# Banded attention followed by a mixture of experts on one core: another opening, with other places, queues and rounds for the loads and the attention stages

## The chip, the core and the metric

The program runs on one core of a Trainium2 chip. The core has five engines, each with its own instruction stream, in order: TensorE (PE in the profile), VectorE (DVE), ScalarE (ACT), GpSimd (POOL) and SyncE (SP, which here only issues DMAs). They meet through semaphores, and transfers run on 16 DMA engines. The metric is device time in microseconds of one execution; the median of several is compared.

## The reference

`q`, `k` and `v` are 4 batches x 8 heads x 576 positions x 64. Heads 0 to 3 see a plain band of 32 positions, heads 4 to 7 a band of 128 with every fourth position:

```python
scores = scale * np.matmul(q, k.transpose(0, 1, 3, 2))
mask_plain = (rel >= 0) & (rel < window)
mask_dil = (rel >= 0) & (rel < window * dilation) & (rel % dilation == 0)
scores = np.where(masks[None, :, :, :], scores, -1000000000.0)
scores = scores - np.max(scores, axis=-1, keepdims=True)
attn = np.exp(scores)
attn = attn / (np.sum(attn, axis=-1, keepdims=True) + 1e-09)
return np.matmul(attn, v)
...
p = domain_probs / (domain_probs.sum(-1, keepdims=True) + 1e-09)
for e in range(E):
    h = np.maximum(x @ w1[e], 0.0)
    out += p[:, e:e + 1] * (h @ w2[e])
```

The attention's output is `x`, 2304 rows of 512 (row = batch and position, column = head and 64). Four experts have `w1` of 512 x 1024 and `w2` of 1024 x 512. All is float32.

## The kernel before

**Attention.** A group (b, p, i) is batch b, pair of heads p (0 and 1 plain, 2 and 3 dilated) and third i of the positions; there are 48. The host sorts positions of the dilated heads so that theirs is a plain band too. `load_qk` brings a group's q [128 x 192] and k [128 x 224] (96 and 112 KB), `load_v` the v windows of a step's groups [128 x 2 x 6 x 64] (192 KB a group). The groups are worked in 25 steps, the first two of one group and the others of two. A step goes through these stages, one in a round n of the main loop, at its lag: `s_qk` (lag 0, PE: 24 small products a group into a PSUM bank each), `s_max` (0, DVE: adds the mask, negates, and takes the row's extreme, three a group, line 285), `s_sub` (1, POOL), `s_exp` (1, ACT), `s_sum` (2, DVE: row sum over 65 columns, the last of which holds 1e-9, and reciprocal), `s_norm` (2, POOL: the product into a tile `pb`), `s_tr` (3, PE: three turns into one bank; ACT copies it out as `pts`, line 340), `s_av` (4, PE: 24 products a group into a bank each; ACT copies them into `x`, line 372). The tuple `stages` (line 378) sets in which order a round issues them: values, turn, scores on PE. The four PSUM places of tag `pa` are taken in rotation by scores, turns and values.

**Experts.** x is cut into three blocks of 768 rows, each in two chunks i of 384 (0 to 5), and w1 and w2 into 16 pieces of 512 KB (`u`). Each float32 operand is held as a high and a low part of a reduced type (`split`: ACT writes the high part, DVE or POOL the difference; `hh`, `hl` for the activations), and a product takes three matmuls in their place. For a visit (u, m) the first product is Strassen's: seven products instead of eight, for which the splits of sums and differences of x (`x_sums`, line 207, DVE, in place in x; `x_part`, the parts B11 to T4) and of w1 (`w1_sums`, POOL) are needed. A visit is a generator that issues 13 pieces: `mm1_b` gives five (S2, S1, S3, S4, A22) on the PSUM banks x and y, then come the next visit's first product in y, three pieces of `mm2` (second half of the rows), the next visit's second product in x, and three `mm2` of the first half. Each `mm2` piece ends in a pass of DVE that adds it into `acc` (line 495). The next visit's A12 product and the last of its five, A22 with T4, both need their bank to be free of what DVE reads of it. There are 47 such visits. Ahead of them stands piece 0 of block 0, which is done in the plain way (`plain`), in two halves of seven pieces each, since the second half of the block's rows exists later; `pause("open")` stands between the two.

**The main loop** (line 713) issues in each round n the loads, the stages, the splits that the table `when` has for n, the loads of weights, and then: below START (10) six filler matmuls (`dummies`, `wt`, which compute nothing and take the same two PSUM banks as `mm2`), from START to OPEN (15) two pieces of the experts, or six fillers while they pause, and from OPEN on PACE (12) pieces. Behind each piece `step()` issues one instruction's worth of the tasks in `queue` (splits and sums of weights and x), which `prepare` fills; `need` issues at once all that is left of a task. START is the round behind the last stage of those groups that block 0's first half needs, OPEN that of its second half. When attention is over, `begin()`, called once in each visit behind its three pieces of the second half, closes attention's tiles and opens wider ones for the experts, and prepares block 2's remaining parts (`x_sums` of chunks 4 and 5 among them). Where the visit that follows is the last of block 0, `need(x_sums, 5)` (line 563) asks for these.

**Queues.** All loads of q, k, the masks and the weights are issued by SP; v of batches 0 and 1 by ACT (line 254), v of batches 2 and 3 by SP; the tile of v has three places, those of q and k six. The shares (`probs`) are loaded as [128 x 18 x 4], and `weigh` normalises them into `pn`.

The functions that the change touches, with what calls them:

## Time and profile before

| | |
|---|---|
| median of 3 executions | 851.78 us (851.03 to 853.73) |
| the profiled execution | 848.25 us |
| its span, first to last instruction | 846.2 us |
| what lies around the span | 2.05 us |
| mean granted clock of TensorE | 0.995 |
| PE busy | 825.4 us, 98% |
| DVE, ACT, POOL busy | 57%, 38%, 48% |
| moved by DMA | 59.17 MB, 70 GB/s over the span |

The span runs from the profile's first instruction to its last; the time of an execution is 2.05 us longer. A share is busy time over the span, a mean over stages that differ. The page also cuts the span into 40 slices of 21 us: PE has 8, 6, 9 and 8 tenths in the first four slices and 9 or more in all later ones but the last, and the transfers' engines have 8, 9 and 8 tenths in the first three and 4 or less behind them.

### The profile page before, as it was taken

The page shows a single profiled execution, that of the slowest core. Times are in us where ns is not written, and L with a number is a line of the kernel's source. Part 1 is how long each engine was busy: PE and PEld are TensorE (multiplying, and loading weights), DVE is VectorE, ACT ScalarE, POOL GpSimd, SP SyncE. Part 2 cuts the span into 40 slices and gives each one's busy share as a digit, 9 for nine tenths or more (in the row PEclk, how much of TensorE's full clock was granted, in tenths as well). Part 3 has the DMA queues.
Part 4 walks back from the last instruction along what each step waited for, and adds up shares of the span by engine and source line. Part 5 has one row for each costly group of instructions (what it writes and reads, how often), then busy time and mean ns, then how long its engine had stood idle before and what let it go on. Part 6 is the DMA issues. An engine that isn't in the chain of part 4 may idle for free.

```text
span 846.2 us, 15635 instructions
## 1 busy us (share of the span) xinstructions
PE 825.4 (98%) x6219; PEld 728.9 (86%) x6219; DVE 482.4 (57%) x1015; ACT 319.5 (38%) x761; POOL 404.6 (48%) x484
## 2 busy tenths in 40 slices
PE   8698999999999999999999999999999999999998
PEld 5477788888888898898898898998998998988986
DVE  4566666568565559645545545555555455455554
ACT  2345544345444455433233242242242232232321
POOL 3466977667676678832332342341341342242210
PEclk9999999999999999999999999999999999999999
DMA  8983432342321221400100101101001001010003
GB/s 230 226 209 90 144 100 90 96 141 76 96 87 51 76 75 50 146 30 26 50 25 26 50 26 35 40 26 50 26 26 51 25 27 50 26 40 12 0 26 125
DMA packets 51464, 59.17 MB, mean 70 GB/s; under 512 B 5952, under 2 KB 40896, under 8 KB 51392
## 3 DMA queue, kind: packets, MB, share of 16 engines
q1 hardware_dynamic: 47936, 53.46, 20.7%
q10 hardware_dynamic: 3456, 4.72, 2.3%
q8 instruction: 49, 0.80, 0.4%
q14 instruction: 23, 0.19, 0.1%
HBM read 53.45 MB, written 4.72 MB: 69 GB/s over the span
## 4 chain that ended last, share of the span: by engine, by line
PE 90%; POOL 3%; DVE 2%; DMA 2%; ACT 1%; issue 1%; SPq 0%; ACTq 0%; POOLq 0%; DVEq 0%
PE m L487 45%; PE m1x L389 23%; PE m1y L389 17%; PE po L356 2%; PE sc L271 1%; PE wt L685 1%; DMA k_s<-kT 1%; PE pt L336 1%; DVE hl L413 1%; DVE xl_T L120 1%; DMA q_s<-qT 0%; POOL g2l L120 0%; POOL g1l L120 0%; DMA v_s<-vw 0%; DVE acc L495 0%
## 5 line engine op out<-in xcount | busy, mean ns | idle before, releaser
L495 DVE SCALAR_TENSOR_TENSOR acc<-m,pn,acc 128x512 f32<-128x512 f32 x270 | 201.8, 749 | 132.6 <-PE m L487 132.3
L487 PE MATMUL m<-w2h,hh 128*128 128x512 f32 x576 | 226.8, 394 | 2.8 <-DVE acc L495 2.3
L487 PE MATMUL m<-w2l,hh 128*128 128x512 f32 x576 | 225.5, 391 | 0.0
L120 POOL TENSOR_TENSOR g2l<-r,g2h 128x256 fp32r<-128x256 f32 x124 | 93.3, 780 | 240.9 <-PE m L487 212.1
L487 PE MATMUL m<-w2h,hl 128*128 128x512 f32 x576 | 178.7, 391 | 0.1
L407 ACT ACTIVATE hh<-s 128x384 fp32r<-128x384 f32 x94 | 49.4, 526 | 248.2 <-DVE s L430 197.8
L487 PEld LDWEIGHTS m<-w2h,hh 128*128 128x128 f32 x576 | 108.1, 188 | 25.4 <-DVE acc L495 4.9
L487 PEld LDWEIGHTS m<-w2h,hl 128*128 128x128 f32 x576 | 108.1, 188 | 24.2 <-DVE hl L413 0.6
L487 PEld LDWEIGHTS m<-w2l,hh 128*128 128x128 f32 x576 | 108.2, 188 | 20.1
L120 POOL TENSOR_TENSOR w2l<-r,w2h 128x512 fp32r<-128x512 f32 x62 | 80.7, 1323 | 45.1 <-ACT w2h L117 44.7
L120 POOL TENSOR_TENSOR g1l<-r,g1h 128x256 fp32r<-128x256 f32 x93 | 69.0, 762 | 68.7 <-ACT g1h L117 68.7
L446 DVE TENSOR_TENSOR s<-m1x,s 128x384 f32<-128x384 f32 x47 | 26.2, 558 | 104.2 <-PE m1x L389 102.6
L439 ACT ACTIVATE u<-m1x 128x384 f32<-128x384 f32 x47 | 23.1, 491 | 144.5 <-PE m1x L389 144.5
L413 DVE SCALAR_TENSOR_TENSOR hl<-s,hh 128x384 fp32r<-128x384 f32 x94 | 60.8, 647 | 28.1 <-ACT hh L407 28.1
L389 PE MATMUL m1x<-xh_T,g2h 128*128 128x384 f32 x156 | 53.0, 340 | 1.8 <-DVE s L430 1.8
L389 PE MATMUL m1x<-xl_T,g2h 128*128 128x384 f32 x156 | 52.8, 338 | 0.0
L389 PE MATMUL m1x<-xh_T,g2l 128*128 128x384 f32 x156 | 52.5, 337 | 0.0
L117 ACT ACTIVATE g2h<-r 128x256 fp32r<-128x256 f32 x125 | 43.4, 406 | 3.9 <-POOL r L149 3.9
L389 PE MATMUL m1y<-xl_B,g2h 128*128 128x384 f32 x128 | 43.1, 336 | 0.0
L389 PE MATMUL m1y<-xh_B,g2h 128*128 128x384 f32 x128 | 43.0, 336 | 0.0
L389 PE MATMUL m1y<-xh_B,g2l 128*128 128x384 f32 x128 | 42.9, 335 | 0.0
L285 DVE CUSTOM_DVE_ANT_0 sm<-sc,mask 128x64 f32<-128x64 f32 x144 | 23.0, 222 | 33.9 <-PE sc L271 27.4
(91 smaller groups left out, 1499.8 us busy)
## 6 DMA issues: line engine op xcount, KB each, us to landing
r<-w SPq DMA_DIRECT2D x64, 512.0 KB, 3.4
k_s<-kT SPq DMA_DIRECT2D x48, 112.0 KB, 3.8
v_s<-vw ACTq DMA_DIRECT2D x24, 192.0 KB, 4.5
q_s<-qT SPq DMA_DIRECT2D x48, 96.0 KB, 4.1
v_s<-vw SPq DMA_DIRECT2D x24, 192.0 KB, 4.0
out<-acc SPq DMA_DIRECT2D x18, 256.0 KB, 2.0
mask<-masks SPq DMA_DIRECT2D x1, 192.0 KB, 4.6
pw<-probs SPq DMA_DIRECT2D x1, 36.0 KB, 6.6
```

The costliest lines, as they stand in the source:

```text
L117: nc.scalar.activation(out=hi, in_=src, func=AF.Copy)
L120: lo_eng.tensor_tensor(out=lo, in0=src, in1=hi.bitcast(F32), op=ALU.subtract)
L271: nc.tensor.matmul(banks[swap][o:o + QB, i * KB:(i + 1) * KB], q_s[h, c0:c0 + QB], k_s[h, c0:c0 + KB], start=True, stop=True, skip_group_c ...
L285: nc.vector.tensor_tensor_reduce(out=sm[:, i * len(gs) + k, :KB], in0=banks[k][:, i * KB:(i + 1) * KB], in1=mask[:, which[blk if p < NP // ...
L356: nc.tensor.matmul(po[k][64 * j:64 * j + 64, o:o + QB], v_s[rows, j, 2 * i + half, :], ts_[rows, c:c + QB], start=True, stop=True,)
L389: nc.tensor.matmul(bank, w[:, k], x[:, k], start=(first and k == 0 and i == 0), stop=(last and k == 1 and i == 2), skip_group_check=True,)
L407: nc.scalar.activation(out=hi, in_=src, func=AF.Relu)
L413: nc.vector.scalar_tensor_tensor(out=lo, in0=src, scalar=0.0, in1=hi.bitcast(F32), op0=ALU.max, op1=ALU.subtract)
L439: nc.scalar.activation(out=u2, in_=x, func=AF.Copy)
L446: nc.vector.tensor_tensor(out=s5, in0=x, in1=s5, op=ALU.add)
L487: nc.tensor.matmul(po, h, w, start=(n == 0 and x == 0), stop=(n == 3))
L495: nc.vector.scalar_tensor_tensor(out=acc, in0=po, scalar=pn[:, tt, e:e + 1], in1=acc, op0=ALU.mult, op1=ALU.add,)
```

## The change

There are 24 steps of two groups. `LAG` is 3: in its own round a step now has scores, maxima, subtraction and exponential, in the next the sum and the product, then the turn, then the values; a round issues scores, values, turn on PE. After the steps that the first half of block 0 needs, and after those that its second half needs, GAP = 3 rounds have no scores (rounds 5 to 7 and 13 to 15), in which the earlier steps' later stages go on. START becomes round 7, OPEN stays round 15, PACE becomes 10. The loads stand in one order: q, k, v and weights on SP's queue, only the first four k and the masks on ACT's; q and k for the groups behind a set of rounds without scores are asked for when those rounds are reached. v has four places. `sm` and `su` are taken in rotation and the product is made in place, without `pb`; the 1e-9 is an instruction of DVE on the sums. The shares are loaded as [18 x 128 x 4], turned on PE in four small transposes, and copied into `pw`. In rounds without scores the filler is three matmuls. The remaining weights' tasks move by a round or two. Computed is the same.

```diff
@@ -19,7 +19,12 @@
 GB = 6
 GS = GB // 2
 GW = GB * QB
-PACE = 12
+PACE = 10
+LAG = 3
+GAP = 3
+QKB = 6
+VB = 4
+FILL = 6
...
-        sms = [ap.tile([128, 2 * GS, KB + 1], F32, name=f"sm{i}", bufs=1) for i in range(3)]
-        for t in sms:
-            nc.gpsimd.memset(t[:, :, KB:], 1e-9)
-
-        def load_qk(b, p, gi):
-            q_s = ap.tile([128, GW], F32, tag="q", name="q_s", bufs=6)
-            k_s = ap.tile([128, GW + WINDOW], F32, tag="k", name="k_s", bufs=6)
+        def load_qk(b, p, gi, k_queue):
+            q_s = ap.tile([128, GW], F32, tag="q", name="q_s", bufs=QKB)
+            k_s = ap.tile([128, GW + WINDOW], F32, tag="k", name="k_s", bufs=QKB)
             nc.sync.dma_start(out=q_s, in_=qT[b, p][:, gi * GW:(gi + 1) * GW])
-            nc.sync.dma_start(out=k_s, in_=kT[b, p][:, gi * GW:(gi + 1) * GW + WINDOW])
+            k_queue.dma_start(out=k_s, in_=kT[b, p][:, gi * GW:(gi + 1) * GW + WINDOW])
             qk_t[b, p, gi] = (q_s, k_s)
 
...
         def load_v(n, gs):
-            t = ap.tile([128, 2, GB, 64], F32, tag="v", name="v_s", bufs=3)
-            queue = nc.scalar if gs[0][0] < 2 else nc.sync
+            t = ap.tile([128, 2, GB, 64], F32, tag="v", name="v_s", bufs=VB)
             for k, (b, p, gi) in enumerate(gs):
-                queue.dma_start(
+                nc.sync.dma_start(
                     out=t[KB * k:KB * (k + 1)], in_=vw[b, p][:, :, gi * GB:(gi + 1) * GB, :]
                 )
             v_of[n] = t
...
-            sm = sms[n % 3]
+            sm = ap.tile([128, 2 * GS, KB], F32, tag="sm", name="sm", bufs=3)
...
-            rc = ap.tile([128, 2 * GS], F32, tag="rc", name="rc", bufs=2)[:, :w]
+            su = ap.tile([128, 2 * GS], F32, tag="su", name="su", bufs=2)
+            rc = ap.tile([128, 2 * GS], F32, tag="rc", name="rc", bufs=2)
             nc.vector.reduce_sum(out=su, in_=sm, axis=mybir.AxisListType.X)
+            nc.vector.tensor_scalar(
+                out=su, in0=su, scalar1=1e-9, scalar2=None, op0=ALU.add
+            )
             nc.vector.reciprocal(out=rc, in_=su)
             st[n] = (sm, rc)
...
         def s_norm(n, gs):
             sm, rc = st[n]
-            w = rc.shape[1]
-            pb = ap.tile([128, 2 * GS, KB], F32, tag="pb", name="pb", bufs=2)[:, :w]
             nc.gpsimd.tensor_tensor(
-                out=pb, in0=sm[:, :, :KB], in1=rc.unsqueeze(2).to_broadcast([128, w, KB]),
+                out=sm, in0=sm, in1=rc.unsqueeze(2).to_broadcast([128, 2 * GS, KB]),
                 op=ALU.mult,
             )
-            st[n] = pb
+            st[n] = sm
...
         def load_masks():
-            nc.sync.dma_start(out=mask, in_=masks)
+            nc.scalar.dma_start(out=mask, in_=masks)
 
 
         stages = (
-            (s_sub, 1), (s_sum, 2), (s_av, 4), (s_tr, 3), (s_norm, 2), (s_exp, 1),
-            (s_qk, 0), (s_max, 0),
+            (s_qk, 0), (s_av, 3), (s_tr, 2), (s_max, 0), (s_sum, 1), (s_sub, 0),
+            (s_norm, 1), (s_exp, 0),
         )
...
+                    assert "m1" in gate
                     need(x_sums, 5)
...
-        steps = [rest[:1], rest[1:2]] + [rest[i:i + 2] for i in range(2, len(rest), 2)]
-        LAG = 4
+        steps = [rest[i:i + 2] for i in range(0, len(rest), 2)]
 
         def done(*gs):
 
-            return LAG + max(n for n, s in enumerate(steps) if any(g in s for g in gs))
+            return LAG + max(at(n) for n, s in enumerate(steps) if any(g in s for g in gs))
+
+        needed = [
+            max(n for n, s in enumerate(steps) if (b, NP - 1, i) in s) for b, i in ((0, 2), (1, 0))
+        ]
+
+        def at(n):
+
+            return n + GAP * sum(n > last for last in needed)
+
+        step_at = {at(n): n for n in range(len(steps))}
...
-        def weigh():
-
+        def load_probs():
+
+            t = wp.tile([NTT, 128, E], F32, tag="w2l", name="pt_", bufs=2)
+            nc.sync.dma_start(out=t, in_=probs.rearrange("(t p) e -> t p e", p=128))
+            return t
+
+        def weigh(t):
+
+            turned = pa.tile([128, 512], F32, tag="pa", name="pe")
+            for e in range(E):
+                nc.tensor.transpose(
+                    turned[:, e * NTT:(e + 1) * NTT], t[:, :, e], ident[:NTT, :NTT]
+                )
+            nc.vector.tensor_copy(
+                pw, turned[:, :E * NTT].rearrange("p (e t) -> p t e", e=E)
+            )
...
-        START = done(*dil(0, 0, 2)) + 1
-        OPEN = done(*dil(1, 0)) + 1
+        START = done(*dil(0, 0, 2))
+        OPEN = done(*dil(1, 0))
         when = {}
         for n, i, names in (
             (done(*plains[0]), 0, ("B11",)), (done(*plains[0]), 1, ("B11",)),
-            (START - 1, 0, ("B21",)), (START - 1, 1, ("B21",)),
+            (START, 0, ("B21",)), (START, 1, ("B21",)),
             (done(*dil(0, 1)), 0, ("X12", "B22", None, "t2", "t1", "t3")),
-            (OPEN - 1, 1, ("X12", "B22", None)),
...
+        qk_done = qk_next = av_done = v_next = 0
+
+        def load_scores(until):
+            nonlocal qk_next
+            while qk_next < min(until, qk_done + QKB, len(flat)):
+                load_qk(*flat[qk_next], nc.scalar if qk_next < 4 else nc.sync)
                 if qk_next == 0:
                     load_masks()
                 qk_next += 1
-            while v_next < len(steps) and v_next < max(n - LAG, 0) + 3 and v_next <= n:
+
+        def load_values(until):
+            nonlocal v_next
+            while v_next < min(until, av_done + VB, len(steps)):
                 load_v(v_next, steps[v_next])
                 v_next += 1
+
+        first = 2 * (needed[0] + 1)
+        dummies(18)
+        ffn = experts(begin)
+        for n in range(at(len(steps) - 1) + LAG + 1):
+            load_scores(first if n <= needed[0] else len(flat))
+            load_values(min(n + 1, qk_done // 2 + 3))
             for stage, lag in stages:
-                if 0 <= n - lag < len(steps):
-                    stage(n - lag, steps[n - lag])
-            if n < len(steps):
-                qk_done += len(steps[n])
+                m = step_at.get(n - lag)
+                if m is not None:
+                    stage(m, steps[m])
+            if n in step_at:
+                qk_done += 2
+            av_done += n - LAG in step_at
...
+            if n == 2:
+                fetch_w1(0)
             if n == 3:
-                fetch_w1(0)
-            if n == 4:
                 fetch_w2(0)
-                nc.sync.dma_start(out=pw, in_=probs.rearrange("(t p) e -> p t e", p=128))
+                shares = load_probs()
             if n == 5:
                 prepare(w1_split, 0)
-            if n == 7:
                 prepare(w2_late, 0)
+            if n == 6:
                 fetch_w1(1)
+            if n == START:
+                weigh(shares)
             if n == START + 1:
-                weigh()
                 prepare(w1_split, 1)
...
             if n < START:
-                dummies(6)
+                dummies(FILL if n in step_at else FILL // 2)
```

**ACT, the rounds in which the first half of the first expert's block is worked.** `hh` are the high parts of that half's activations, `g1h` the high parts of w1's second piece, whose tile is `r_651` in after and `r_723` in before; `w2h` is of w2. Before:

```order
L372 ACTIVATE xr<-po 128x4x48 x2
L340 ACTIVATE pts<-pt 128x384
L309 ACTIVATE sm_94<-sm_94 128x6x64
L117 ACTIVATE xh_T_0_1373<-xr 128x2x192
L117 ACTIVATE xh_T_0_1389<-xr 128x2x192
L117 ACTIVATE xh_T_0_1393<-xr 128x2x192
L117 ACTIVATE g1h<-r_723 128x256
```

After:

```order
L122 ACTIVATE w2h<-r_424 128x512
L306 ACTIVATE sm<-sm 128x384
L403 ACTIVATE hh<-m1x 128x384
L122 ACTIVATE g1h<-r_651 128x256
L403 ACTIVATE hh<-m1y 128x384
L122 ACTIVATE g1h<-r_651 128x256
L306 ACTIVATE sm<-sm 128x384
L122 ACTIVATE g1h<-r_651 128x256
```

The first `g1h` of w1's second piece stands between the two `hh` of the first half now; before it stood behind both and three more rounds.

**PE, a round among the experts.** `sc` are scores, `po` values, `pt` the turn; m1x and m1y are products of the experts, `xh_...` high parts of x. Before:

```order
L389 MATMUL m1x<-xh_T_0_1373,g2l 128x384
L389 MATMUL m1x<-xl_T_0_1374,g2h 128x384
L356 MATMUL po<-pts,v_s 64x32 x24
L336 MATMUL pt<-ident,pb 128x128 x3
L271 MATMUL sc<-k_s,q_s 32x64 x24
L389 MATMUL m1y<-xh_T_0_1389,g2h 128x384
L389 MATMUL m1y<-xh_T_0_1389,g2l 128x384
```

After:

```order
L385 MATMUL m1y<-xh_T_0_1225,g2l 128x384
L385 MATMUL m1y<-xl_T_0_1226,g2h 128x384
L271 MATMUL sc<-k_s,q_s 32x64 x24
L352 MATMUL po<-pts,v_s 64x32 x24
L332 MATMUL pt<-ident,sm 128x128 x3
L385 MATMUL m1x<-xh_T_0_1229,g2h 128x384
L385 MATMUL m1x<-xh_T_0_1229,g2l 128x384
```

The scores moved from behind the turn to the head of the round.

**DVE, where attention ends and block 2's x is prepared.** `xl_B_2` are low parts of x for block 2, `xr<-xr` the sums of x (line 207 before, 212 after), `acc` the additions behind `mm2`, `s` and `u` the sums that free banks x and y (line 446 before is 442 after). Before:

```order
L446 TENSOR_TENSOR s_4652<-m1x,s_4652 128x384
L207 TENSOR_TENSOR xr<-xr 128x2x192
L450 TENSOR_TENSOR u_4651<-m1y,u_4651 128x384
L413 SCALAR_TENSOR_TENSOR hl<-s_4652,hh 128x384
L413 SCALAR_TENSOR_TENSOR hl<-u_4651,hh 128x384
L207 TENSOR_TENSOR xr<-xr 128x2x192
L413 SCALAR_TENSOR_TENSOR hl<-m1x,hh 128x384
L207 TENSOR_TENSOR xr<-xr 128x2x192 x2
L495 SCALAR_TENSOR_TENSOR acc_1260<-m_4727,pn,acc_1260 128x512
L207 TENSOR_TENSOR xr<-xr 128x2x192
L495 SCALAR_TENSOR_TENSOR acc_1260<-m_4740,pn,acc_1260 128x512
L207 TENSOR_TENSOR xr<-xr 128x2x192
```

After:

```order
L426 TENSOR_TENSOR s_4680<-m1x,s_4680 128x384
L409 SCALAR_TENSOR_TENSOR hl<-s_4680,hh 128x384
L125 TENSOR_TENSOR xl_B_2_4753<-xr,xh_B_2_4752 128x2x192
L125 TENSOR_TENSOR xl_B_2_4759<-xr,xh_B_2_4758 128x2x192
L125 TENSOR_TENSOR xl_B_2_4765<-xr,xh_B_2_4764 128x2x192
L212 TENSOR_TENSOR xr<-xr 128x2x192 x8
L491 SCALAR_TENSOR_TENSOR acc_851<-m_4778,pn,acc_851 128x512
L491 SCALAR_TENSOR_TENSOR acc_851<-m_4790,pn,acc_851 128x512
L491 SCALAR_TENSOR_TENSOR acc_851<-m_4804,pn,acc_851 128x512
L442 TENSOR_TENSOR s_4815<-m1x,s_4815 128x384
L446 TENSOR_TENSOR u_4814<-m1y,u_4814 128x384
L409 SCALAR_TENSOR_TENSOR hl<-s_4815,hh 128x384
```

The eight sums, which stood among a visit's passes, stand in one run behind three low parts, ahead of three `acc` and the sum `s`.

## Rows read from the trace of the kernel before

**Rows 1.** Head of the page: span, busy time, share and instructions of each engine.

```profile
span 846.2 us, 15635 instructions
...
PE 825.4 (98%) x6219; PEld 728.9 (86%) x6219; DVE 482.4 (57%) x1015; ACT 319.5 (38%) x761; POOL 404.6 (48%) x484
```

**Rows 2.** Stretches: from:to, length, busy us (instructions), PE clock, DMA share, GB/s.

```profile
0.00:10.00 10.00, 8.55 (x134) 4.93 (x135) 2.42 (x26) 1.65 (x2) 2.35 (x12) 1.00 0.79 204
...
30.00:40.00 10.00, 7.37 (x256) 5.28 (x257) 6.23 (x32) 5.89 (x17) 4.94 (x5) 1.00 0.96 246
...
40.00:66.00 26.00, 24.88 (x654) 19.07 (x652) 18.90 (x100) 13.22 (x37) 15.76 (x18) 1.00 0.82 209
...
80.00:90.00 10.00, 10.00 (x136) 9.36 (x135) 7.04 (x22) 7.08 (x19) 9.06 (x10) 0.83 0.63 181
```

**Rows 3.** PE's waits, whole span: line, releaser: us in total, times, longest.

```profile
PE sc L271 <- ACT xr L372: 7.3, 7, 3.7
PE m L487 <- DVE acc L495: 2.3, 2, 1.8
PE m1x L389 <- DVE s L430: 1.8, 1, 1.8
```

**Rows 4.** PE in time, three moments: start, us, instruction, count [idle before, releaser].

```profile
25.49 0.81 PE L271 MATMUL sc<-k_s,q_s 64*32 64x64 f32 x44 [3.73 <-ACT xr L372]
...
43.24 0.44 PE L389 MATMUL m1x<-xh_B,g1h 128*128 128x384 f32 x1
...
65.96 0.44 PE L389 MATMUL m1x<-xh_T,g1h 128*128 128x384 f32 x1
```

**Rows 5.** ACT in time, 20 to 26 us (ACTq: its queue issuing).

```profile
20.72 4.34 ACTq L256 DMA_DIRECT2D v_s<-vw  x2
...
25.55 0.50 ACT L340 ACTIVATE pts<-pt 128x384 f32<-128x384 f32 x1
```

**Rows 6.** PE in time, fillers and one round among the experts.

```profile
62.38 1.04 PE L685 MATMUL wt<-ident 128*128 128x256 bf16 x6
...
84.14 0.90 PE L356 MATMUL po<-pts,v_s 64*64 64x32 f32 x48
84.97 0.55 PE L336 MATMUL pt<-ident,pb 128*128 128x128 f32 x3
85.45 0.72 PE L271 MATMUL sc<-k_s,q_s 64*32 64x64 f32 x48
86.10 0.45 PE L389 MATMUL m1y<-xh_B,g2h 128*128 128x384 f32 x1
```

**Rows 7.** PE in time, three pieces' starts in a steady visit.

```profile
293.30 0.39 PE L487 MATMUL m<-w2h,hh 128*128 128x512 f32 x1
...
301.66 0.34 PE L389 MATMUL m1x<-xh_T,g1h 128*128 128x384 f32 x1
...
302.73 0.33 PE L389 MATMUL m1y<-xh_B,g1h 128*128 128x384 f32 x1
```

**Rows 8.** DVE in time, the same visit.

```profile
294.72 0.56 DVE L413 SCALAR_TENSOR_TENSOR hl<-s,hh 128x384 fp32r<-128x384 f32 x1 [0.59 <-ACT hh L407]
...
303.35 1.09 DVE L413 SCALAR_TENSOR_TENSOR hl<-u,hh 128x384 fp32r<-128x384 f32 x1
...
304.37 0.54 DVE L413 SCALAR_TENSOR_TENSOR hl<-m1x,hh 128x384 fp32r<-128x384 f32 x1
```

**Rows 9.** Line 207: shortest/median/longest ns, first and last start.

```profile
L207 DVE TENSOR_TENSOR xr<-xr x24: 540/609/1107, 50.8 to 329.6; 128x384 f32<-128x384 f32 x24
```

**Rows 10.** DVE by line: count, busy us, mean ns, idle before and releaser.

```profile
L495 DVE SCALAR_TENSOR_TENSOR acc<-m,pn,acc 128x512 f32<-128x512 f32 x270 | 201.8, 749 | 132.6 <-PE m L487 132.3
...
L285 DVE CUSTOM_DVE_ANT_0 sm<-sc,mask 128x64 f32<-128x64 f32 x144 | 23.0, 222 | 33.9 <-PE sc L271 27.4 <-PE wt L685 6.4
...
L657 DVE TENSOR_SCALAR ps__69<-ps__69 128x18 f32<-128x18 f32 x1 | 0.8, 829 | 0.0
```

**Rows 11.** POOL by line, the same columns.

```profile
L301 POOL TENSOR_TENSOR sm<-sm,nm 128x384 f32<-128x384 f32 (+1 forms) x25 | 21.1, 846 | 17.9 <-DVE nm L285 16.4 <-DVE ps__69 L656 1.4
```

22 lines of the change are left out of this document (6 added, 16 removed).

## The prediction

> **What bounds the kernel now.** I read the page's first lines, then the stretches, the waits of PE, PE's own timeline, and last the queues. PE is busy 825.4 of 846.2 us [rows 1], so a gain must take PE work away, fill PE's gaps, or replace the filler matmuls (`wt`), which count as busy and compute nothing. The granted clock is 1.00 nearly everywhere; 80 to 90 us shows 0.83 [rows 2], which costs 1.7 us if PE has work all through it.
>
> Two moments divide the run. At 43.24 PE issues the first expert product, at 65.96 the first of the second half of the first expert's block [rows 4]. Until then it is attention, filler, seven expert pieces and waits; afterwards the experts always have work, and 846.2 - 65.96 = 780.2 us follow. So the question is when that second moment comes, and what it leaves to be done.
>
> Of 20.8 us of idle PE, 7.3 are scores waiting for ACT's copy of an attention result [rows 3]. The longest, 3.73 us before 25.49 [rows 4], shows the cause: ACT had been held 4.34 us from 20.72 by two v loads that it issues itself, so its copies came late [rows 5]. The 16 DMA engines stand at a share of 0.96 from 30 to 40 us, at 246 GB/s [rows 2]. The opening is bound by transfers, and by engines that stand behind them in order.
>
> After 65.96 PE idles little: 1.8 us for DVE's sum at line 430, 2.3 us in two waits for `acc` [rows 3].
>
> **The change, part by part.** *Bytes before the second moment.* A group is 96 KB of q, 112 of k and 192 of v by the tiles' shapes; masks are 192 and a piece of w1 or w2 is 512. The new SP order puts 7780 KB (7.97 MB: 16 groups of q and k, seven pairs of v, masks, w1 twice, w2 once, shares) up to the end of w1's second piece, and 9892 KB (10.13 MB) up to the scores' twentieth group. By 10 us before has moved 2.04 MB; at 0.246 MB/us [rows 2] these land at 10 + 5.93/0.246 = 34.1 and at 42.9 us.
>
> *The first half.* v of pair 4 (5252 KB) lands at 23.6 by the same rate; its values and the turned shares follow, so the first product comes near 25 instead of 43.24.
>
> *What stops it.* ACT's new order has the first copy of w1's second piece between the two `hh` of the first half. From about 31 ACT stands there until 34.1, and the first `mm2` needs the second `hh`. Add 0.4 for that copy, 0.5 for `hh` (both by ACT's 0.50 us passes [rows 5]) and the semaphores: PE goes on at 35.1. From here the rounds are bound by engines. Round 9: two `mm2` pieces, 2.4 us, to 37.5. Round 10: scores 0.65, turn 0.48 [rows 6], the third piece 1.4, to 40.3; the filler behind it shares its two banks with the expert sums, and the third `acc` stands on DVE behind two `acc` (0.75 each), six maxima (1.33) [rows 10] and a row sum (0.56, as DVE's other passes over as many numbers [rows 8]), so the filler ends at 42.3. Rounds 11 and 12: scores, values 0.83, turn, six fillers 1.04 [rows 6], 3.1 each with the semaphores, to 48.4. Round 13 waits for the normalised pair 8 on POOL, which first splits x (four passes, 0.85 each by its own subtraction [rows 11]): to 51.1. Round 14: 2.3, to 53.4. Round 15: values to 54.3, two copies and a split on ACT, 1.2: the second moment is at **55.5**. Lower bound: data alone, 42.9 and then one pair's chain with nobody ahead of it: on PE 0.65, 0.48 and 0.83 [rows 6], six maxima 1.33, a row sum and two small passes 1.2, POOL's two passes 1.7, five of ACT 2.6 and 0.6 for semaphores, 9.4 in all: 52.3. Upper: loads at 209 GB/s, what 40 to 66 us had [rows 2], put w1 at 38.4 and the moment near 60.
>
> *What is left.* Before had issued scores of 16 of 25 steps, values of 12 and turns of 13. After has ten pairs of 24 through all three. That leaves five scores (0.65), one set of values (0.83) and two turns (0.48) more [rows 6], and 0.1 at a change of shape: 5.1 us.
>
> *The round's order.* Scores, values, turn replaces values, turn, scores. The four PSUM places rotate, so the turn takes the place of the scores of its own round and waits for DVE's maxima of them. In the fill DVE is free. Among the experts it is behind by what it owes: 1.5 us after a round's start the turn is ready, and the last two of its three maxima need 0.45 [rows 10] once DVE is free. In a steady visit DVE frees at 304.91 if the round starts at 302.73, at 304.44 if at 301.66, at 295.28 if at 293.30 [rows 7, 8]: stalls of 1.1, 1.7 and 0.9. The order shows each of these three starts once among the 11 rounds that have scores and a turn, the other eight behind a free DVE: 3.7 us. Bounds: 0, since DVE may be earlier with less work of x beside it, and 5.5.
>
> *Ten pieces a round instead of twelve.* Attention ends 180 pieces after the second moment instead of 168. A visit has 13, so the late pools open in visit 13, not 12, and `need(x_sums, 5)` asks for all of block 2's x at that very point. DVE gets three x splits and eight subtractions in one run, ahead of three `acc` and the sum that frees bank x. PE needs that bank 301.66 - 293.30 = 8.36 us after the opening product [rows 7]. DVE is free 2.0 after that product (295.28 against 293.30 [rows 7, 8]); three splits, like its 1.09 us passes there, last to 5.2; eight subtractions at 0.83, near the middle between the median 0.609 and the longest 1.107 [rows 9], to 11.8; three `acc`, overlapping likewise, 2.0; the sum 0.56: 14.4. PE stands 6.0 us. Bounds: subtractions at 0.47 (0.54 long [rows 9], less the 0.07 by which passes overlap [rows 8]) give 3.2; at 1.07, 8.0. Before spread the same work over a visit and lost 0.5. Net 5.5.
>
> *Small things.* The added 1e-9 is an instruction on DVE a pair: between 0.22 (a maximum) and 0.83 (line 657's, on 18 columns) [rows 10], 24 of them, 5 to 20 us of DVE, beside expert matmuls, where DVE has 40% free; in the fill it lies in the chain and I take 0.1 of each. The turned shares add four small turns, 0.5 us, inside the wait for ACT. v loads leave ACT: with ACT's wait above counted, that is in the 55.5. The 1.75 us wait for `acc` near 99 and one of 0.26 should go, since block 1's x is now split later and among fewer tasks: -2.0.
>
> **Sum**, on the profiled execution: 55.5 + 780.2 + 5.1 + 3.7 + 5.5 - 2.0 = 848.0 us of span, 1.8 above 846.2. What lies around the span (848.25 - 846.2) stays. The median of the runs is 851.78, 3.5 above the profiled execution; 1.8 on it gives **853.6**. A measurement of this kernel can tell about 0.3%, 2.6 us, from no change, so the forecast is no change, leaning to slower: the opening gains 10.5 us and pays 12.3.
>
> **Rivals.** *A: the opening's gain stays.* The fill runs at the pace of data (52.3) and DVE's run stalls PE by its lower bound (3.2, net 2.7): 52.3 + 780.2 + 5.1 + 3.7 + 2.7 - 2.0 = 842.0, median near 847.5, and 844 if the turns do not wait either. For it: rounds in the fill are short of work, DMA is the row with the highest share. Against: ACT, DVE and POOL run strictly in order and the new order puts x and weight pieces between attention's.
>
> *B: slower, by DVE's run at the end of attention.* Eleven two-input passes on DVE against a POOL that works all through that stretch: 8.0 (net 7.5), and a fall of the clock behind so long a gap, 1.7 us as at 80 to 90 [rows 2], and turns at 5.5: 55.5 + 780.2 + 5.1 + 5.5 + 7.5 + 1.7 - 2.0 = 853.5, median 859. It decides from a stall of about 7 us at that place. For it: these subtractions took from 540 to 1107 ns [rows 9]. Against: POOL too may have to wait for its weights there. The Trainium skill ("SBUF — State Buffer", Who interferes with whom) has a rule that sharpens this: a DVE instruction with two SBUF inputs and a GpSimd instruction that reads SBUF exclude each other for whole instructions. By it each of the eleven could wait for a whole POOL pass, an estimate of 10 us or more of stall, and the sum would be 858 or so; the longest, 1107 ns, is only 0.57 above the shortest [rows 9], less than one POOL pass of 0.85 [rows 11], so the rule in its full size is not seen here.
>
> *C: one queue carries less than two.* At 209 GB/s the moment is at 60, the sum 852.5, median 858. Against: with SP alone loading, 80 to 90 us moved 181 GB/s at a share of 0.63 [rows 2], 287 at a full share. The Trainium skill ("DMA: Bandwidth & Descriptors", Issuing engines are not separate DMA queues) says that all issuers end on the same 16 engines, and by it the number of queues changes no time here; the trace of before has no saturated stretch of one queue to show it.
>
> **Chances.** Forecast 0.42 (849 to 857 its own range), A 0.33, B 0.18, C 0.07. The forecast's range lies 0.65 within 0.3%, 0.27 above, 0.08 below; A is faster but for a tenth or so; B and C are slower. Together: faster 0.33, same 0.31, slower 0.36. The range takes A down to 841, for a DVE run that costs nothing on top of turns that don't wait (844 - 2.7), and B up to 860.
>
> **What would show it.** First product near 25, second moment near 55: if at 52 or sooner, A's fill. A PE gap of some 4 us near 31 to 35 behind ACT's `hh`: if absent, the step on ACT is wrong. Turns waiting for DVE in about three rounds. One gap of about 6 us near 260 to 280 before the product of A22 and T4, with eight line 212 passes on DVE: if it is under 3, that term is wrong. A SP queue that waits for PE's places while the DMA share is low would make the data's times wrong.

## The result, and the profile after

The changed kernel takes **864.25 us** (863.17 to 865.63, 4 runs) against 852.75 (851.03 to 855.20, 4 runs) of the kernel before: a ratio of 1.0134, 95% interval [1.0102, 1.0165]. It is slower by 11.5 us; forecast was no change, 853.6, with a range from 841 to 860. The profiled execution, the shortest of the four, took 863.17, its span is 861.4.

The page's head, to be read beside [rows 1]:

```profile
span 861.4 us, 15613 instructions
...
PE 826.0 (96%) x6214; PEld 730.7 (85%) x6214; DVE 493.5 (57%) x1038; ACT 321.1 (37%) x759; POOL 400.7 (47%) x479
```

PE is as busy as before. The 15.2 us of span that are added are idle time or time at a lower clock. The two parts that the prediction cut the run into, each a row (from:to, length, busy us of PE, PEld, DVE, ACT and POOL, clock, DMA share, GB/s), before:

```profile
0.00:65.96 65.96, 54.78 (x1420) 39.06 (x1420) 36.60 (x219) 26.89 (x71) 31.02 (x45) 0.97 0.87 220
65.96:846.20 780.24, 770.63 (x4805) 689.79 (x4800) 445.75 (x797) 292.63 (x691) 373.55 (x439) 1.00 0.18 57
```

and after:

```profile
0.00:62.02 62.02, 51.08 (x1120) 37.09 (x1121) 33.10 (x173) 25.74 (x65) 29.83 (x41) 0.89 0.77 206
62.02:861.40 799.38, 774.90 (x5094) 693.60 (x5094) 460.39 (x866) 295.32 (x695) 370.86 (x439) 0.99 0.18 58
```

The second half of the first block starts at 62.02, 3.94 us sooner. What follows takes 799.4 in place of 780.2, 19.2 us more: PE is idle for 24.5 us of it in place of 9.6. Counted in stretches of 2 us, as busy time times clock, PE's work there is 772.7 us in place of 768.9, and the lower clock (busy time less work) costs 2.2 in place of 1.7: 3.8 + 14.9 + 0.5 = 19.2.

PE's waits after, as [rows 3]:

```profile
PE m1x L385 <- DVE s L442: 7.7, 1, 7.7
PE pt L332 <- DVE nm L285: 6.3, 6, 1.6
PE pt L332 <- POOL sm L321: 3.2, 4, 1.5
PE m L483 <- ACT hh L403: 2.7, 2, 2.1
PE m1y L385 <- ACT s L439: 2.1, 1, 2.1
```

The scores' 7.3 us behind ACT's copies are gone. In their place stand one wait of 7.7 us, six of turns for DVE (6.3), and turns waiting for POOL's products. PE in time at the moments of [rows 4]:

```profile
28.72 0.69 PE L385 MATMUL m1x<-xh_B,g1h 128*128 128x384 f32 x1
...
39.63 0.50 PE L483 MATMUL m<-w2h,hh 128*128 128x512 f32 x1 [2.12 <-ACT hh L403]
...
62.02 0.44 PE L385 MATMUL m1x<-xh_T,g1h 128*128 128x384 f32 x1 [1.05 <-ACT xh_T L122]
```

The first product comes 14.5 us sooner, the second half only 3.9. Between them ACT, as foreseen, stands for w1's second piece between the two `hh`:

```profile
36.26 0.47 ACT L403 ACTIVATE hh<-m1x 128x384 fp32r<-128x384 f32 x1
38.78 0.42 ACT L122 ACTIVATE g1h<-r 128x256 fp32r<-128x256 f32 x1 [2.06 <-DMA r<-w]
39.11 0.47 ACT L403 ACTIVATE hh<-m1y 128x384 fp32r<-128x384 f32 x1
```

It stood until 38.78 where 34.1 was forecast, and PE stood 2.12 us, until 39.63. SP had issued that load here (SPq is its queue issuing):

```profile
32.21 0.59 SPq L107 DMA_DIRECT2D r<-w  x1
```

In and behind gaps in PE's work the clock is down. Three stretches of the opening (columns as above):

```profile
20.00:30.00 10.00, 7.66 (x136) 6.21 (x129) 5.05 (x12) 6.41 (x18) 3.06 (x4) 0.68 0.84 210
30.00:40.00 10.00, 7.88 (x122) 6.40 (x121) 3.79 (x19) 2.13 (x6) 1.84 (x4) 0.81 0.93 238
40.00:50.00 10.00, 9.72 (x174) 6.65 (x173) 7.67 (x47) 2.42 (x7) 7.75 (x12) 0.83 0.63 178
```

Half of full speed, 1.2 GHz, is granted from about 23 to 33 us and from 41 to 44; before it was so only for some 3 us near 27.

The 7.7 us wait is DVE's run behind the end of attention, at 339 to 347 us; the prediction looked for it near 260 to 280. DVE, then POOL, then PE there:

```profile
336.13 8.09 DVE L212 TENSOR_TENSOR xr<-xr 128x384 f32<-128x384 f32 x8
344.14 2.05 DVE L491 SCALAR_TENSOR_TENSOR acc<-m,pn,acc 128x512 f32<-128x512 f32 x3
346.12 0.54 DVE L442 TENSOR_TENSOR s<-m1x,s 128x384 f32<-128x384 f32 x1
```

```profile
336.75 1.05 POOL L125 TENSOR_TENSOR g2l<-r,g2h 128x256 fp32r<-128x256 f32 x1
337.77 3.05 POOL L125 TENSOR_TENSOR g1l<-r,g1h 128x256 fp32r<-128x256 f32 x3
340.89 0.92 POOL L150 TENSOR_TENSOR r<-r 128x256 f32<-128x256 f32 x1
```

```profile
346.71 0.69 PE L385 MATMUL m1x<-xh_T,g1h 128*128 128x384 f32 x1 [7.67 <-DVE s L442]
```

Eight sums take 8.09 us, 1.01 each, while POOL runs without a break (three more sums of w1 follow the last row), and three `acc` and the sum `s` that frees bank x stand behind them. Then PE works at half clock for some 4 us; the stretch around it:

```profile
344.00:352.00 8.00, 5.29 (x17) 5.07 (x18) 4.71 (x9) 2.59 (x6) 1.80 (x2) 0.57 0.00 1
```

### The profile page after: what moved, and what is told of

Same layout as the page of the kernel before. It is cut to its first block, busy times and chain, and to the rows that moved or that the text cites. A ratio compares the mean times of both kernels' runs of the same rounds, so it can differ in the third digit from the quotient of the medians.

```text
span 861.4 us, 15613 instructions
## 1 busy us (share of the span) xinstructions
PE 826.0 (96%) x6214; PEld 730.7 (85%) x6214; DVE 493.5 (57%) x1038; ACT 321.1 (37%) x759; POOL 400.7 (47%) x479
## 4 chain that ended last, share of the span: by engine, by line
PE 88%; DVE 5%; DMA 2%; issue 2%; POOL 1%; ACT 1%; SPq 1%; ACTq 0%; DVEq 0%; POOLq 0%
PE m L483 44%; PE m1x L385 22%; PE m1y L385 17%; PE sc L271 1%; PE po L352 1%; DVE xr L212 1%; PE pt L332 1%; DMA v_s<-vw 1%; DMA r<-w 1%; DVE acc L491 1%; PE wt L705 1%; DVE xl_T L125 1%; DVE sm L285 1%; DVE hl L409 1%; DMA k_s<-kT 0%
## 5 line engine op out<-in xcount | busy, mean ns | idle before, releaser
L125 POOL TENSOR_TENSOR g2l<-r,g2h 128x256 fp32r<-128x256 f32 x124 | 91.3, 761 | 248.0 <-PE m L483 213.5
L409 DVE SCALAR_TENSOR_TENSOR hl<-s,hh 128x384 fp32r<-128x384 f32 x94 | 57.5, 612 | 28.0 <-ACT hh L403 27.8
L385 PE MATMUL m1x<-xh_T,g1h 128*128 128x384 f32 x96 | 33.3, 347 | 8.7 <-DVE s L442 7.7
```

The source lines that it names most:

```text
L125: lo_eng.tensor_tensor(out=lo, in0=src, in1=hi.bitcast(F32), op=ALU.subtract)
L385: nc.tensor.matmul(bank, w[:, k], x[:, k], start=(first and k == 0 and i == 0), stop=(last and k == 1 and i == 2), skip_group_check=True,)
L409: nc.vector.scalar_tensor_tensor(out=lo, in0=src, scalar=0.0, in1=hi.bitcast(F32), op0=ALU.max, op1=ALU.subtract)
```

## The experiments

Each kernel ran against the one before on the same chip. "2nd half" is the start of the second half of the first expert's block and "rest" what follows, both in the profiled execution. The median of before was 852.75 us beside the change and 850.7 to 851.0 beside the others, so kernels are compared by their ratios, and under some 0.3% they are not told apart. The 852.75 is the median of four executions only. Against 850.8 the change would stand at 1.016, so a gain over it may be larger than the ratios say.

e1 and e5 issue the same instructions as the change up to the second half, and yet theirs starts at 61.6 and 60.2 where the change's starts at 62.0. One execution's start therefore says nothing of a difference under some 2 us. In the same way the lower clock just behind that start cost nothing in the change's profiled execution and 1.6 to 4.8 us in those of e1, e4, e5, e13 and e14, which is in their "rest".

| kernel | median us | ratio to before, 95% | 2nd half | rest |
|---|---|---|---|---|
| the change | 864.25 | 1.0134 [1.0102, 1.0165] | 62.0 | 799.4 |
| e1_pace9 | 858.60 | 1.0096 [1.0073, 1.0119] | 61.6 | 795.3 |
| e2_turn_first | 873.98 | 1.0280 [1.0254, 1.0306] | 65.3 | 808.5 |
| e3_fill12 | 865.36 | 1.0165 [1.0143, 1.0186] | 61.4 | 799.4 |
| e4_w1_later | 861.02 | 1.0114 [1.0091, 1.0137] | 60.3 | 800.4 |
| e5_pool_free | 863.20 | 1.0146 [1.0113, 1.0178] | 60.2 | 800.1 |
| e6_no_add | 866.34 | 1.0169 [1.0146, 1.0193] | 64.7 | 800.5 |
| e7_gap0 | 858.86 | 1.0098 [1.0079, 1.0116] | 66.1 | 788.8 |
| e8_v_act | 869.12 | 1.0208 [1.0184, 1.0233] | 64.8 | 798.6 |
| e9_gap1_w1 | 854.22 | 1.0037 [1.0019, 1.0055] | 65.3 | 788.8 |
| e10_no_pause_fill | 867.82 | 1.0183 [1.0150, 1.0217] | 60.8 | 800.7 |
| e11_pace9_w1_nofill | 854.98 | 1.0041 [1.0022, 1.0060] | 59.7 | 793.1 |
| e12_before_v_sp | 849.94 | 0.9982 [0.9962, 1.0002] | 67.0 | 781.6 |
| e13_w1_early | 864.04 | 1.0139 [1.0106, 1.0173] | 60.5 | 802.9 |
| e14_gap1 | 854.29 | 1.0038 [1.0025, 1.0051] | 63.7 | 788.9 |
| e15_gap1_w1_early | 855.45 | 1.0059 [1.0037, 1.0081] | 65.4 | 786.1 |
| e16_before_k_act | 850.07 | 0.9986 [0.9972, 1.0000] | 65.8 | 781.3 |
| e17_before_queues_shares | 846.90 | 0.9947 [0.9928, 0.9966] | 65.8 | 781.6 |
| e18_before_shares | 850.22 | 0.9985 [0.9969, 1.0002] | 66.7 | 781.7 |

**The run on DVE.**

```diff
-PACE = 10
+PACE = 9
```

> The changed kernel with 9 pieces of the experts a round in place of 10, nothing else. Attention then ends 162 pieces after the second half begins, so the late pools open in visit 12, and the eight sums of block 2's x stand one by one among a visit's passes, as in the kernel before. Theory T (the run on DVE costs it): the 7.7 us wait of PE for the sum at line 442 falls below 1 us, the halved clock behind it (346.7 to 351 us) goes, and of the 864.25 us about 9 go: 853 to 857. Rival R (DVE and POOL are simply behind with the same work, and denser rounds put more of it in less time): the wait comes back as waits for acc, the maxima or low parts; 861 to 866.

By the ratio it is 0.38% or 3 us below the change, with intervals that overlap, where T had 9. The sums stand among a visit's passes again and the 7.7 us wait is gone (1.1 us in two waits for line 442 are left), but denser rounds bring others; PE's waits:

```profile
PE pt L332 <- DVE nm L285: 4.1, 4, 1.8
PE m1x L385 <- ACT u L435: 3.3, 1, 3.3
PE pt L332 <- POOL sm L321: 3.0, 3, 1.5
```

T holds for the wait; the time lies between the two ranges.

```diff
-            split(gh[:, i], gl[:, i], a, nc.scalar, nc.gpsimd if u else nc.vector)
+            if u == 16:
+                nc.scalar.activation(out=gh[:, i], in_=a, func=AF.Copy)
+                nc.scalar.activation(out=gl[:, i], in_=a, func=AF.Copy)
+            else: ...
...
+        if u == 16:
+            return
```

> The changed kernel without POOL's work for piece 16 of w1 (three low parts and four sums); ACT writes copies in the place of the low parts, and the sums are left out, so that part of the values is left out. In the changed kernel this work stands beside the eight sums of block 2's x on DVE, which take 1.01 us each. Theory T (DVE's two-input passes and POOL's shut each other out): the eight sums take 0.5 to 0.6 each, PE's 7.7 us wait falls to 3.5 to 4.5, and the time from 864.25 to 859 to 861.5. Rival R (the sums are slow in themselves, as they follow one another in place): they stay at 0.9 or more, and the wait at 7 or more, time 863 to 865.

The passes of DVE one by one (line 218 here is 212 after), and POOL beside them:

```profile
335.82 1.08 DVE L218 TENSOR_TENSOR xr<-xr 128x384 f32<-128x384 f32 x1
336.94 0.98 DVE L218 TENSOR_TENSOR xr<-xr 128x384 f32<-128x384 f32 x1
...
338.02 0.56 DVE L218 TENSOR_TENSOR xr<-xr 128x384 f32<-128x384 f32 x1
...
339.67 1.25 DVE L218 TENSOR_TENSOR xr<-xr 128x384 f32<-128x384 f32 x1
...
340.95 0.56 DVE L218 TENSOR_TENSOR xr<-xr 128x384 f32<-128x384 f32 x1
```

```profile
335.43 2.06 POOL L125 TENSOR_TENSOR g2l<-r,g2h 128x256 fp32r<-128x256 f32 x2
339.21 1.29 POOL L125 TENSOR_TENSOR xl_B<-xr,xh_B 128x384 fp32r<-128x384 f32 x1 [1.71 <-ACT xh_B L122]
```

A sum takes 0.56 us where POOL stands still (338.02, 340.95) and 0.98 to 1.25 where POOL is at a pass when it starts. PE's wait fell from 7.7 to 4.0. T is shown for the passes. The time did not follow (1.0146, not told from the change's 1.0134). PE got a new gap of 1.9 us in the same visit, as a copy of x now stood on ACT ahead of its copy `s` and waited for one of DVE's sums:

```profile
338.61 0.52 ACT L122 ACTIVATE xh_B<-xr 128x384 fp32r<-128x384 f32 x1 [2.27 <-DVE xr L218]
```

And the lower clock cost 4.8 us in the rest in place of 2.2: 3.2 of it still between 300 and 400 us, 1.6 just behind the second half's start.

**The turns.**

```diff
-            (s_qk, 0), (s_av, 3), (s_tr, 2), (s_max, 0), (s_sum, 1), (s_sub, 0),
+            (s_av, 3), (s_tr, 2), (s_qk, 0), (s_max, 0), (s_sum, 1), (s_sub, 0),
```

> The changed kernel with the order of a round's PE work of the kernel before: values, turn, scores, where the change has scores, values, turn; lags and rounds are kept. Theory T (the turn takes the PSUM place of its own round's scores and stands behind their maxima on DVE): the six waits of turns for DVE, 6.3 us in all, fall to under 1.5, and the time from 864.25 to 857 to 860. Rival R (whichever stage comes last in the round takes the place that the rotation frees last): the scores wait for ACT's copies of the values instead, as the 7.3 us of the kernel before, mostly in the opening; 862 to 867.

Both theories fell: 1.0280, 1.5% slower than the change. The turns wait for DVE no more, as T said, but PE's waits read:

```profile
PE m1x L385 <- DVE s L442: 9.2, 3, 7.7
PE pt L332 <- POOL sm L321: 8.7, 6, 2.2
PE m1y L385 <- ACT s L439: 3.0, 2, 2.0
PE m1x L385 <- ACT u L435: 2.3, 2, 1.6
PE m L483 <- DVE acc L491: 2.1, 3, 1.1
```

In the stretch where the change's turns waited, PE is idle as long as before: 7.9 us from 104 to 338, and 7.3 from 100 to 326 after. What the turns no longer wait, the experts' products wait behind DVE and ACT (`s`, `u`, `acc`): PE meets DVE's debt at another place. That says why nothing is won. Of the 12.4 us of span that are lost, 3.3 lie ahead of the second half, where POOL's products are later; 3.9 are a lower clock behind it (6.1 in place of 2.2), 0.5 are idle time, and 4.7 are longer busy times of the same 5094 instructions, which no row here takes apart.

```diff
-            nc.vector.tensor_scalar(
-                out=su, in0=su, scalar1=1e-9, scalar2=None, op0=ALU.add
-            )
```

> The changed kernel without the instruction that adds 1e-9 to a step's row sums (24 of them, median 0.45 us, from 0.17 to 0.88); the 1e-9 is left out. Theory D (it lies in the chain from maxima to product in the opening, and DVE is what the turns wait for later): the turns' 6.3 us of waits for DVE fall to 3 to 5, their 3.2 us for POOL to 1 to 2, and the time from 864.25 to 859.5 to 862. Rival H (the instruction stands where DVE has time): 863 to 865.5.

1.0169, not less: H, though 866.34 is above H's range too. The turns' waits for DVE are 6.7. The added instruction is not a cause.

**The opening.**

```diff
-            if n == START + 1:
+            if n == START + 4:
                 prepare(w1_split, 1)
                 prepare(w1_sums, 1)
```

> The changed kernel with the tasks for w1's second piece (three copies on ACT, three low parts and four sums on POOL) prepared three rounds later, in round 11 in place of 8. Theory T (ACT's stand before that piece's landing holds the second hh, PE's 2.1 us gap at 39.6 and the lower clock from 40 to 47 follow from it, and POOL's low parts and sums delay attention's passes): the gap goes, the second half of the block begins at 57 to 60 in place of 62.0, and the time is 859 to 862. Rival R (the opening hangs on attention's own chain and on the loads): the gap goes, but the second half begins at 61 to 63, and the time stays at 863 to 866.

```diff
+            if n == 4:
+                fetch_w1(1)
...
-            if n == 6:
-                fetch_w1(1)
```

> The changed kernel with w1's second piece loaded in round 4 in place of 6, so that on SP it stands ahead of the q and k that wait for places. Theory L (that piece's landing at 38.4 is what makes the second half late): it lands by 30, PE's 2.1 us wait at 39.6 goes, the second half starts at 57 to 59.5 in place of 62.0, time 859 to 861.5. Rival K (the rounds of attention in between are as long as their chain through PE, DVE, POOL and ACT): the wait goes, but the second half starts at 60 to 62.5, time 861.5 to 865.

In both PE's wait at 39.6 is gone, and in both the second half starts only 1.5 to 1.8 us sooner, at 60.3 and 60.5, no more than e5 without such an edit. Neither ratio is told apart from the change's; e4's time lies in T's range and e13's in K's. That the rounds of attention behind it set the rest (K) is not shown, for these rounds ran at a lower clock than the change's. From 50 to 60 us e4, then after (e13 has 0.66 there too):

```profile
50.00:60.00 10.00, 7.75 (x164) 5.70 (x162) 4.11 (x8) 5.41 (x16) 7.95 (x10) 0.66 0.83 225
50.00:60.00 10.00, 8.20 (x224) 5.97 (x222) 7.06 (x25) 6.57 (x18) 7.55 (x9) 1.00 0.73 198
```

e4's values of round 14 start at 54.15, 3.0 us ahead of after's 57.19; at the second half 1.8 of that are left. Behind that start the lower clock cost 5.0 us in e4 and 7.2 in e13, in place of 2.2; why is open.

```diff
-                dummies(FILL if n in step_at else FILL // 2)
+                dummies(12 if n > 2 else FILL)
```

> The changed kernel with 12 filler matmuls in each of rounds 3 to 6 (3 or 6 there now), nothing else. Its granted clock is half from 22.9 to 33 us and from 40.7 to 44, behind waits of PE for v and for hh; that takes 6.5 us of the opening. Theory C (the clock falls for too little work on PE in these rounds): the clock from 20 to 33 us is 1.00 for most of it, the second half starts at 58 to 60 in place of 62.0, time 860 to 862.5. Rival F (the clock falls behind the waits whatever PE does ahead of them, and fillers only take time): the stretch of half clock stays, the second half starts at 62 to 66, time 864 to 868.

Stretch 20 to 30 us:

```profile
20.00:30.00 10.00, 10.00 (x191) 7.32 (x190) 5.24 (x13) 6.56 (x19) 3.20 (x5) 1.00 0.88 234
```

The clock is back at 1.00 (0.68 after; 0.50 and 0.82 in e1 and e5, whose opening is the same), and the start of the second half moves by 0.7 us, the time not to the better. So C is right on the clock and wrong on its price. What PE gained it lost at the next wait: it stood 2.83 us for `hh`, until 39.04, behind the same piece of w1. The fuller rounds together with an earlier or later w1 were not run.

```diff
                 if next(ffn) == "idle":
-                    dummies(FILL)
```

> The changed kernel without the six filler matmuls in each round in which the experts pause (rounds 10 to 14); the fillers below START stay. Theory P (in these rounds PE itself is what a round's length hangs on: 2.8 to 3.6 us, 1.0 to 1.9 of them filler): the second half starts at 57 to 60 in place of 62.0, time 859 to 862. Rival K (the rounds hang on the chain through DVE, POOL and ACT, and without filler the clock falls): it starts at 61 to 64, the clock from 45 to 62 us shows 0.5 to 0.8, time 863 to 867.

K: the second half at 60.8, turns wait 5.9 us for POOL's products in place of 3.2, the clock from 50 to 60 us is 0.56, and the ratio is 1.0183.

```diff
+            queue = nc.scalar if gs[0][0] < 2 else nc.sync
...
-                nc.sync.dma_start(
+                queue.dma_start(
```

> The changed kernel with the loads of v of batches 0 and 1 issued by ACT, as in the kernel before; the rest of the order on SP, and the four places, are kept. Theory Q (an engine that issues and waits for a place or for the ring stands still with its copies behind it): scores and turns wait for ACT's copies again, 3 us or more in the opening, the second half starts at 63 to 67, and the time is 865 to 870. Rival S (in the changed kernel v and weights stand on SP behind q and k that wait for PE to free their places, so w1's second piece lands at 38.4 and not at 34): that piece lands by 36, the second half starts at 59 to 61, and the time is 860 to 863.

Q: 1.0208, the second half at 64.8. PE waited 4.55 us at 23.77 for a copy by ACT, which had been held:

```profile
17.33 6.02 ACTq L257 DMA_DIRECT2D v_s<-vw  x2
```

**The rounds without scores.**

```diff
-GAP = 3
+GAP = 0
```

> The changed kernel with GAP = 0: no rounds without scores, all else kept. Scores go on behind the steps that block 0's halves need; OPEN moves from round 15 to 12, and attention ends 150 pieces behind it in place of 180, so the late pools open in visit 11 and the eight sums spread over a visit. Theory T: the 7.7 us wait and the low clock behind it go (about 9.5 us), the leftover of attention behind the second half's start falls by some 3 us, and the second half starts at 61 to 65 in place of 62.0, since two pairs' scores stand ahead of the first product on queue and engines: 850 to 857. Rival R: the scores' loads and DVE's maxima put the start of the second half at 67 or later, and the time at 858 to 865.

The second half starts at 66.1, as PE waits 6.9 us for a k that stands behind weights, but the rest takes 788.8 in place of 799.4. 858.86 lies in R's range, though T was right on the rest.

The same with `GAP = 1`, alone, with e4's edit, and with e13's:

> The changed kernel with one round without scores in place of three (GAP = 1), nothing else. Theory T (the 5.2 us wait for x at the start of the second half, seen with GAP = 1 and the later w1, came from POOL's low parts of w1 ahead of a subtraction, and an exponential on ACT behind that ahead of x's copies): the second half starts at 60 to 63, what follows takes 787 to 790, time 849 to 853. Rival R (with a pair's scores in every round but one, its exponential stands ahead of x's copies anyhow): it starts at 64 to 67, time 853 to 857.

> The changed kernel with one round without scores in place of three (GAP = 1), and w1's second piece prepared three rounds later. Attention ends 160 pieces behind the second half's start, in visit 12, so the eight sums of block 2's x are spread. From the runs so far: the second half starts at 62 to 66 (66.1 with GAP = 0, where PE waited 6.9 us for k; 60.3 with GAP = 3 and the later piece), what follows takes 788 to 792 us (788.8 with GAP = 0, 799.4 with GAP = 3). Theory T (the leftover of attention and the run decide): span 850 to 855, median 853 to 858. Rival R (PE waits for k behind the weights' loads as with GAP = 0, and what follows is as long as with 9 pieces, 795): span 858 or more, median 861 or more.

> GAP = 1 and w1's second piece loaded in round 4, on the changed kernel. Theory T (both gains add up): second half at 59 to 62, time 847 to 851.5. Rival R (w1 now stands ahead of the k for which PE waited 4.5 us with GAP = 1, and the wait grows by its 2 us): second half at 63 to 66, time 852 to 856.

1.0038, 1.0037 and 1.0059: 0.75 to 0.97% or 6 to 8 us below the change. In e14 the two parts read

```profile
0.00:63.68 63.68, 48.06 (x1207) 35.54 (x1207) 35.09 (x200) 25.38 (x65) 30.17 (x42) 0.89 0.79 222
63.68:852.60 788.92, 775.81 (x4998) 694.86 (x4998) 454.97 (x839) 294.87 (x695) 371.11 (x438) 0.99 0.18 57
```

PE is idle 13.1 us in the second, in place of 24.5. The eight sums stand among a visit's passes here, from 308.8 to 320.5, so the 7.7 us wait and the half clock behind it are gone with the rounds: e14 does not separate the two. But the second half starts 1.7 us later, behind a wait of 4.9 us for x. ACT and POOL ahead of it:

```profile
59.38 0.53 ACT L368 ACTIVATE xr<-po 128x192 f32<-128x192 f32 x2
62.70 0.52 ACT L306 ACTIVATE sm<-sm 128x384 f32<-128x384 f32 x1 [2.79 <-POOL sm L299]
63.12 0.51 ACT L122 ACTIVATE xh_T<-xr 128x384 fp32r<-128x384 f32 x1
```

```profile
59.55 0.72 POOL L125 TENSOR_TENSOR g1l<-r,g1h 128x256 fp32r<-128x256 f32 x1 [0.94 <-ACT g1h L122]
60.35 0.72 POOL L150 TENSOR_TENSOR r<-r 128x256 f32<-128x256 f32 x1
61.15 0.72 POOL L152 TENSOR_TENSOR r<-r 128x256 f32<-128x256 f32 x1
61.83 0.83 POOL L299 TENSOR_TENSOR sm<-sm,nm 128x384 f32<-128x384 f32 x1
```

POOL subtracts for the exponential (61.83) behind a low part and two sums of w1, and x's copy stands behind that exponential. That is R of e14: with a round's scores an exponential stands ahead of x's copies, and with e9's later w1 the wait is 5.2. In e15 the wait for k grew to 6.1 (2.9 in e14, 4.5 in e9), as its R had it.

Three edits at once (9 pieces, e4's, e10's):

> Three edits on the changed kernel at once: 9 pieces a round, w1's second piece prepared three rounds later, no fillers while the experts pause. The first two alone gave 5.7 and 3.2 us. Theory T (they concern different places and add up, the third gives 2 or more): 851 to 855. Rival R (the start of the second half comes earlier, but block 0's and block 1's x are then late, and PE waits among the experts for what it did not wait for at the start): 856 to 860.

854.98, the upper end of T: the second half at 59.7, the rest 793.1. So with all three rounds without scores kept, 1.0041 is as low as e14's 1.0038.

**Parts of the change on the kernel before.** v on SP; that with the first four k and the masks on ACT; the shares turned on TensorE; all of these:

> The kernel before with one part of the change: v of batches 0 and 1 is loaded by SP in place of ACT; three places for v as before, order of the rest kept. Theory Q (ACT held by two v loads makes the scores wait 7.3 us for its copies): those waits fall under 3 us, the second half starts at 61 to 64 in place of 66.0, and of the median of before 2 to 5 us go. Rival S (SP waits for v's place instead, with q and k behind it, since there are only three): scores wait for k, the second half starts at 65 to 68, and the time is as before or up to 3 us more.

> The kernel before with the change's queues alone: v on SP, the first four k and the masks on ACT; order, places, stages and pieces as before. v on SP alone gave 0.998 of before. Theory Q (the first scores start sooner and nothing later is touched): 1 to 3 us less than with v on SP alone, 846.5 to 849.5. Rival N (the opening's length hangs on bytes, and the first 10 us are made up for later): 849.5 to 852.

> The kernel before with the change's way with the shares alone. Theory Z: 1 to 3 us less than before, by the same transfers; the 3.7 us wait near 25 shrinks. Rival N: no difference within 1 us, 850 to 852.

> The kernel before with the change's queues (v on SP, first four k and masks on ACT) and the change's way with the shares (loaded as 18 rows, turned by four transposes on TensorE in round 8). Theory Z (the shares' 2304 pieces of 16 bytes hold the transfers up, while v is waited for 3.7 us at 26.5): that wait falls under 2, and the time to 846 to 849. Rival N (36 KB are too few to matter): 849 to 851.5, as with the queues alone.

With v on SP alone the waits for ACT's copies fell to 0.3 us, and 4.5 for v and 2.6 for k came (S). Each of the first three is within 0.2% of before, with 1 at or just inside the end of its interval: not told from no change. Together they give 846.90, 0.9947 [0.9928, 0.9966], faster than both kernels; the queues and the shares by themselves would make 0.9986 x 0.9985 = 0.9971, which their intervals do not tell from it. In e16 PE waited 4.4 us for v; in e17

```profile
PE po L356 <- DMA v_s<-vw: 2.0, 2, 1.2
```

2.0 us are left, as Z said. The profiled execution of e17 was one of its slower ones (849.19), with the second half at 65.8, so its trace does not show where the 3.9 us come from.

## Why the prediction was wrong

The forecast's span was 848.0, the measured one is 861.4: 6.5 us more ahead of the second half and 6.9 behind its start.

- *The second half at 55.5* failed, by 6.5, and 62.0 is above its upper bound of 60. The step on ACT was right, but w1's piece landed 4.7 us late, and PE went on at 39.63 where 35.1 was forecast: 4.5 of the 6.5. The forecast took bytes to land in the order of the queue at 246 GB/s. By 38.8 some 8.7 MB had moved, an estimate from 205 GB/s to 10 us and 232 behind it, where the sum has 7.97 up to that piece; so loads issued behind it landed ahead of its end. The sign that the prediction named, a SP queue that waits for PE's places, is hardly there: from 10 to 33 us SP waited 1.0 us for PE and 3.4 for landings. The other 2.0 are the rounds from there on, which took 22.4 us where 20.4 was forecast: two turns waited 0.82 and 0.63 for POOL's products, at 55.85 and 58.72, and PE ran at half clock from 41 to 44. Fuller PE (e3), no filler (e10) and another w1 (e4, e13) each gave 0.7 to 1.8, within what the same opening differs by from one execution to the next, and each met another wait or a lower clock. In e4 PE goes on without a wait at 36.72, and the rounds take 23.5, the last of them at the lower clock. How much of the 6.5 would go with the piece and the clock both put right, and how much is the chain through POOL, DVE and ACT, is open.
- *Leftover of attention 5.1*: the counts were right (five scores, one set of values and two turns more), and PE's work grew by 3.8.
- *Turns 3.7*: six waits, not three, 6.3 us, above the bound of 5.5. The mechanism was read right and its size wrongly. The order is not to be charged with it: in e2, without this order, PE is idle as long.
- *DVE's run 6.0, net 5.5*: the mechanism and the place among the instructions were right, the size was 7.7, by sums of 1.01 us in place of 0.83, and the half clock behind it cost 2.2 more. The time of 260 to 280 us was wrong; the last of these sums stands at 329.6 in [rows 9] already. This was rival B, which asked for a stall of 7 us and more, and I gave it 0.18. Its span of 853.5 with 62.0 for 55.5 is 860.0; 861.4 was measured. That it comes so near is in part luck: the leftover and the clock cost less than it had, and its -2.0 came out at about +1.4.
- *-2.0 for waits that go*: they went, but 2.06 at 82.37 for `s` on ACT, 0.61 at 63.24, 0.50 at 155.29 and 0.63 at 336.85 came. The 1.69 at 76.08 is the 1.8 that before had for the same sum.

So behind the second half's start the terms that were too small are the turns (by 2.6), the run (by 1.7), the waits that came (by 3.4) and the clock (0.5, put at nothing), and the leftover was 1.3 too large. The rounds without scores push scores, maxima and sums in among the experts. With one in place of three 8 us come back (e14), but part of that is the run on DVE, which goes with them and was worth some 3 us where it went alone (e1), and three edits that keep these rounds give as much (e11). What the rounds cost by themselves is not shown.

## What to carry to other kernels

An opening is not shorter because its first product comes sooner: look at when the last input of the next stage is ready, and at what was put off into the stage that was full. Where a task list is emptied at a fixed point, follow which iteration that point falls into; one piece a round more or less decides whether the work is spread or stands in one run. A wait that an order causes may be a debt of the engine waited for: take the order back before the gain is counted. And see first how far a moment moves between executions with the same instructions ahead of it (60.2 to 62.0 here) before an edit is credited with moving it.

## What the hardware showed

A two-input pass of DVE over 128 x 384 takes 0.56 us beside an idle POOL and 0.98 to 1.25 beside a busy one (e5), and 1.01 on the mean of eight in a row (after). The Trainium skill ("SBUF — State Buffer", Who interferes with whom) says that such passes of the two engines contend for a shared pair of ports, under an exclusive lock. The prediction took the rule as not seen in its full size. The rows agree with its direction, and still not with its full size: in the run one sum of DVE and one pass of POOL start every 1.02 us, while alone they take 0.56 and 0.73 (POOL's passes over 128 x 256 with DVE at rest, after), 1.29 in all.

The added 1e-9, one input of 128 x 6, took 0.17 us in three of its 24 times, two of them with hardly a POOL pass beside it, and 0.44 to 0.53 in 19 that lay almost wholly beside one (after). A small pass of DVE took up to three times its shortest length there.

With fuller rounds PE's clock was 1.00 from 20 to 30 us (e3), where three executions with the change's opening had 0.50 to 0.82, and the time did not get better.
